# Attention in a fused kernel: scores in batches of four blocks instead of two, with the matmul banks divided anew and the row sums moved by ScalarE

## The chip, the cores and the metric

The kernel runs on one core of a Trainium2 chip. The metric is the device time of the whole program in microseconds (us). The engines are named as the profile names them: PE is TensorE (matmuls), DVE is VectorE, ACT is ScalarE, POOL is GpSimd, and SP issues most DMA transfers. Each engine works through its own instructions in program order and waits for the others by semaphores.

## The reference, cut to what matters

```
scores = (1/8) * q @ k^T               # 2 batches, 12 heads, 448 rows, 64 wide
scores = cap * tanh(scores / cap)
attn   = exp(scores - max) / (sum(exp(scores - max)) + 1e-9)
x      = attn @ v                      # as 896 rows of 768
x      = relu(x @ w_in)^2 @ w_out      # 768 -> 2048 -> 768
out    = silu(x @ w2_in) @ w2_out
```

In the path that runs here the cap bounds the scores, so no maximum is taken off: exp is applied to cap * tanh as it is.

## The kernel before, in words

The program has two parts: the attention (about the first 87 us) and two feed-forward layers on the result. The order of the attention's instructions is written out in one loop of `attention_bounded`; the feed-forward's comes from a planner with costs and due times, and is the same instruction list in both kernels.

Heads go in pairs. Pair i = 2m + b is the two heads of head-pair m in batch b, so there are 12 pairs and 6 values of m. Keys are cut in blocks: for each m there are A0, A1, A2 (128 keys each of pair 2m), B0, B1, B2 (the same of pair 2m + 1) and C (the last 64 keys of both pairs). These are 42 blocks, in the order A0 A1 A2 C B0 B1 B2 for m = 0 to 5. For each block

- `scores` (L640) makes the transposed scores in two banks of PSUM (one per head), and ACT applies tanh to both, 128 x 896 numbers, into a tile e (L648; eight such tiles);
- ACT applies exp in place (L744);
- `values` (L659) multiplies by v and adds up over the four blocks of a pair in a bank px;
- `add` (L673, L675, L679) adds the e tiles of a pair on DVE into a tile total.

When a pair is complete, DVE copies px to its cell x_c (L701, `evacuate`). When both pairs of an m are, PE sums the two totals over the keys with a matmul against ones (L687, `add_up`), DVE copies those sums out (L705), and they go through DMA: to 32 partitions (L708), inverted on DVE (L711, L712), written to a scratch in HBM (L713) and fetched back spread out (L719). Then DVE multiplies the cell by them (L724, `normalise`) and POOL splits the cell at once into two float16 parts, high (L1531) and low (L1532), in the tile x0f. The last two pairs, 10 and 11, take a shorter way: PE makes their sums spread out already (L696, tiles sump), and DVE adds, inverts and multiplies (L731 to L733, `last_sums`).

The loop takes two blocks per step h: scores and tanh of the two, exp of the two, then on DVE and PE the adds and values of the two blocks before. A list `todo` holds the later steps of the sums with the step at which they are due. In between, `ws.step()` issues the preparation of feed-forward weights (L360 to L393).

[...] Before, four are two pairs of banks for scores and four are single banks shared by px and the sums.

The feed-forward begins with `plain`, whose first product ha_0f reads batch 0 of x0f. Its loops run over `r` (two halves), the parts (high by high, high by low, low by high) and the cells; for batch 0 they read the cells in this order: c0 and c4 (six matmuls), then c2 and c6 (six matmuls), with weights hl_0, then the same with hl_1 and the same for batch 1 (ha_1f: c1, c5, c3, c7). c8 and c10 come after these 48 matmuls. So the eighth matmul of ha_0f is the first to read the high part of c6, and the tenth the first to read its low part.

Of the kernel before, what the change touches and what calls it, by code (L numbers as in the profile page):

```python
# [26 lines left out]
def softcap_attention_relu2_silu(  # L27
# [47 lines left out]
    work = ctx.enter_context(tc.tile_pool(name="work", bufs=1))  # L75
    psum = ctx.enter_context(tc.tile_pool(name="psum", bufs=2, space=PSUM))

    dram = ctx.enter_context(tc.tile_pool(name="dram", bufs=1, space=bass.MemoryType.DRAM))

    def bank(name):  # L80
        return psum.tile([128, 512], F32, tag="p", bufs=4, name=name)
# [7 lines left out]
    ib, ip = idle.bitcast(BF16), bank("idle")  # L89
    for _ in range(20):  # L90
        nc.tensor.matmul(ip[:, :256], lhsT=ib[:, :128], rhs=ib[:, :256], start=True, stop=True)

# [507 lines left out]
    def attention_bounded(att, spool, ws, x0):  # L600
# [21 lines left out]
        scratch = dram.tile([NH, S], F32, tag="scratch", name="scratch")  # L622
        ex, total, px, sums, st, rb = {}, {}, {}, {}, {}, {}

# [9 lines left out]
        def scores(m, x):  # L634
            sp = bank2(spool, f"s{m}_{x}")
# [12 lines left out]
            nc.scalar.activation(t, sp[:, :, :S], AF.Tanh, scale=scale_s)  # L648

        def values(m, x):  # L650
            for i in (2 * m, 2 * m + 1) if x == "C" else (pair_of(m, x),):
                if i not in px:
                    px[i] = bank(f"px{i}")
            e = ex[m, x]
            for b in range(2) if x == "C" else (None,):
                for j in range(2):
# [5 lines left out]
                        rhs=e[:, j] if b is None else e[head(b), j],  # L662
                        start=x == "A0" or b == 1,
                        stop=x == "B2" or b == 0,
                    )

        def add(m, x):
            e, i = ex[m, x], None if x == "C" else pair_of(m, x)
            if i == NP2 - 1:
                return  # L670
            if x in ("A1", "B1"):
# [4 lines left out]
            if x in ("C", "B1"):  # L676
                b = int(x == "B1")
                t = total[2 * m + b][head(b)]
                nc.vector.tensor_tensor(t, t, ex[m, "C"][head(b)], op=ALU.add)  # L679

        def add_up(m):

            s = sums[m] = bank(f"sum{m}")
            for b in range(2):
# [6 lines left out]
        def add_up_pair(i, t, start=True, stop=True, part=slice(0, 128)):  # L691

            if start:
                sums["p", i] = bank(f"sump{i}")
            for j in range(2):
# [40 lines left out]
        todo, last = [], 2 * NQ - 2  # L736
        loads = {0: 0, 2: 1, 4: 2, 7: 3, 11: 4, 16: 5}
        groups = [blocks[n : n + 2] for n in range(0, len(blocks), 2)]
        for h in range(len(groups) + 1):
            if h < len(groups):  # L740
                for m, x in groups[h]:
                    scores(m, x)
                for m, x in groups[h]:
                    nc.scalar.activation(ex[m, x], ex[m, x], AF.Exp, scale=scale_c)  # L744
                for m, x in groups[h]:
                    if x in ("A0", "B0"):
                        i = pair_of(m, x)
                        if i + 2 < NP2:
                            pr.load_v(i + 2)
                    if x in ("A1", "C") and m + 1 < NQ:  # L750
                        pr.load(2 * m + 2 + (x == "C"))
            if h == 1:
# [4 lines left out]
                nc.vector.tensor_scalar(gcap, gcap, 1e-9 * ONE, None, op0=ALU.mult)  # L757
            older = groups[h - 2] if h > 1 else []
            for m, x in older:
                if x in ("C", "B2"):  # L760
                    evacuate(2 * m + (x == "B2"))
            for m, x in groups[h - 1] if h else []:
                add(m, x)
            for m, x in groups[h - 1] if h else []:
                values(m, x)
            for m, x in groups[h - 1] if h else []:
                if m == NQ - 1 and x in ("C", "B0", "B1", "B2"):
                    add_up_pair(
                        last + 1, ex[m, x], x == "C", x == "B2", head(1) if x == "C" else slice(0, 128)
                    )  # L770
                if m == NQ - 1 and x == "C":
                    add_up_pair(last, total[last])
            for m, x in older:
# [7 lines left out]
            if h in loads:  # L781
                ws.load_to(loads[h])
            for f, at in list(todo):
                if h >= at:
                    f()
                    todo.remove((f, at))
            if 5 <= h < 17:
                ws.step()
        for st_ in last_sums(last):
            st_.fn()  # L790
        for f, _ in todo:
# [4 lines left out]
    def attention_general(att, spool, ws, x0):  # L796
# [8 lines left out]
        for i in range(NP2):  # L805
            pr.load(i)
            pr.load_whole_v(i)
            for j in range(2):
# [7 lines left out]
                for g in range(2):  # L816
                    sp = bank2(spool, f"sg{n}_{g}")
                    for e in range(2):
# [786 lines left out]
    def run(attention, tag, dt):  # L1605
        narrow = dt == F16
        power = POWER if narrow else dict.fromkeys(POWER, 0)
        with ExitStack() as pools:
# [25 lines left out]
            with (  # L1634
                tc.tile_pool(name=f"att{tag}", bufs=2) as att,
                tc.tile_pool(name=f"s{tag}", bufs=2, space=PSUM) as spool,
            ):
                attention(att, spool, ws, x0)
            qpool = pools.enter_context(tc.tile_pool(name=f"q{tag}", bufs=4, space=PSUM))
# [65 lines left out]
```

## Time and profile before

| | us |
|---|---|
| median of 3 runs | 495.69 (495.53 to 495.81) |
| profiled execution: its time | 496.47 |
| profiled execution: span of the trace | 494.70 |
| busy in the span: PE, DVE, ACT | 484.2, 427.2, 363.9 |

The span runs from the first to the last event in the trace. The 1.77 us between it and the execution's time lie around it. PE is busy 98% of the span, but that share counts a matmul as busy from its issue to its modelled end, so small pauses between matmuls of different shapes lie inside it.

### The profile page before, as it was taken

What the parts mean: (1) busy time and instruction counts of PE and PEld (TensorE: products, weight loads), DVE (VectorE), ACT (ScalarE), POOL (GpSimd) and SP (SyncE); (2) the same over time, 40 slices, a digit from 0 to 9 for tenths busy, and PEclk for the clock granted to TensorE, in tenths of its full rate; (3) what the DMA queues carried; (4) which work ended last, traced back from release to release, by engine and by line L of the source; (5) the groups of instructions that cost most, each with busy time, mean ns of one, the idle gap of its engine ahead of it and who ended that gap; (6) DMA issues with size and microseconds to landing.
All of it is one profiled execution on the core that took longest, in us unless ns stands there. A gap on an engine that the chain in (4) does not pass through costs nothing.

```text
span 494.7 us, 7120 instructions
## 1 busy us (share of the span) xinstructions
PE 484.2 (98%) x2563; PEld 233.5 (47%) x2563; DVE 427.2 (86%) x772; ACT 363.9 (74%) x592; POOL 49.2 (10%) x46
## 2 busy tenths in 40 slices
PE   8999999999999999999999999999999999998995
PEld 4323333455555555555555554555555445554552
DVE  0778998998999998999998999999967799988663
ACT  5999996899979935999987878779754689871100
POOL 1001555302002000112200000100010000000000
PEclk9999999999999999999999999999999999999998
DMA  7746561343653113337751333303745733033024
GB/s 246 280 133 164 182 197 30 91 161 134 204 192 129 64 65 127 130 127 237 273 192 64 129 128 129 97 32 127 259 180 152 272 130 127 1 112 112 1 78 154
DMA packets 22386, 69.76 MB, mean 141 GB/s; under 512 B 2886, under 2 KB 14150, under 8 KB 22342
## 3 DMA queue, kind: packets, MB, share of 16 engines
q1 hardware_dynamic: 22308, 69.22, 42.3%
q8 instruction: 22, 0.36, 0.3%
q14 instruction: 22, 0.18, 0.1%
q0 software_dynamic: 32, 0.00, 0.0%
q10 hardware_dynamic: 2, 0.00, 0.0%
HBM read 63.64 MB, written 5.54 MB: 140 GB/s over the span
## 4 chain that ended last, share of the span: by engine, by line
PE 92%; ACT 3%; DMA 2%; DVE 1%; issue 0%; SPq 0%; ACTq 0%
PE p_0df L932 8%; PE px L659 7%; PE p_6df L932 4%; PE p_2bf L932 4%; PE s_B L640 3%; PE s_A L640 3%; PE ha_0f L932 3%; PE yb_5f L932 3%; PE yb_0f L932 3%; PE yb_1f L932 3%; PE yb_3f L932 3%; PE yb_4f L932 3%; PE yb_2f L932 3%; PE ha_1f L932 3%; PE p_4df L932 2%; DMA yf<-spill 2%
## 5 line engine op out<-in xcount | busy, mean ns | idle before, releaser
L648 ACT ACTIVATE e_A<-s_A 128x896 f32<-128x896 f32 x18 | 15.9, 918 | 4.7 <-PE s_A L640 4.5
L648 ACT ACTIVATE e_B<-s_B 128x896 f32<-128x896 f32 x18 | 15.9, 917 | 3.9 <-PE s_B L640 3.6
L744 ACT ACTIVATE e_B<-e_B 128x896 f32<-128x896 f32 x18 | 16.5, 953 | 0.0
L744 ACT ACTIVATE e_A<-e_A 128x896 f32<-128x896 f32 x18 | 16.5, 954 | 0.0
L1434 DVE SCALAR_TENSOR_TENSOR yf<-p_6df,yf 128x448 f32<-128x448 f32 x15 | 9.2, 623 | 6.1 <-PE p_6df L932 6.1
L679 DVE TENSOR_TENSOR total<-total,e_C 64x896 f32<-64x896 f32 x11 | 12.9, 1173 | 0.4
L882 DVE TENSOR_TENSOR yaf<-p_2bf,yaf 128x448 f32<-128x448 f32 x15 | 9.3, 621 | 1.1 <-PE p_2bf L932 1.0
L1434 DVE SCALAR_TENSOR_TENSOR yf<-p_4df,yf 128x448 f32<-128x448 f32 x15 | 9.1, 618 | 0.0
L391 ACT ACTIVATE hl_107f<-u_86f 128x768 f16<-128x768 f32 x1 | 0.8, 843 | 11.1 <-DVE u_86f L416 11.1
L218 DVE SCALAR_TENSOR_TENSOR x1f<-yaf,x1f 128x448 f16<-128x448 f32 x12 | 7.4, 620 | 1.5 <-ACT x1f L871 1.5
L675 DVE TENSOR_TENSOR total<-total,e_A 128x896 f32<-128x896 f32 x6 | 8.2, 1359 | 0.3
L882 DVE TENSOR_TENSOR yaf<-yaf 128x448 f32<-128x448 f32 x12 | 7.1, 621 | 1.1 <-ACT yaf L871 1.0
L673 DVE TENSOR_TENSOR total<-e_A,e_A 128x896 f32<-128x896 f32 x6 | 7.4, 1242 | 0.4 <-ACT e_A L744 0.4
L871 ACT ACTIVATE x1f<-yaf 128x448 f16<-128x448 f32 x12 | 6.8, 570 | 0.7 <-DVE yaf L882 0.5
L360 POOL CAST zeros<-raw_wd_2f 128x768 f16<-128x768 bf16 x1 | 1.1, 1056 | 63.1 <-DVE u_55f L365 63.1
L757 DVE TENSOR_SCALAR gcap<-gcap 128x1 f32<-128x1 f32 x1 | 0.2, 154 | 7.6 <-ACT gcap L756 7.6
L673 DVE TENSOR_TENSOR total<-e_B,e_B 128x896 f32<-128x896 f32 x5 | 6.5, 1294 | 0.0
L1434 DVE SCALAR_TENSOR_TENSOR yf<-c_6df,yf 128x448 f32<-128x448 f32 x3 | 1.9, 624 | 4.9 <-PE c_6df L932 4.9
L391 ACT ACTIVATE hr_50f<-u_66f 128x384 f16<-128x384 f32 x1 | 0.5, 522 | 7.5 <-PE p_0df L932 7.5
L732 DVE RECIPROCAL r<-r 128x448 f32<-128x448 f32 x2 | 5.9, 2953 | 0.1
L675 DVE TENSOR_TENSOR total<-total,e_B 128x896 f32<-128x896 f32 x5 | 5.5, 1091 | 0.4
L360 POOL CAST zerosf<-raw_wa15f 128x768 f16<-128x768 bf16 x1 | 1.3, 1329 | 45.1 <-DVE u_27f L365 45.1
(1808 smaller groups left out, 1676.0 us busy)
## 6 DMA issues: line engine op xcount, KB each, us to landing
yf<-spill SPq DMA_DIRECT2D x12, 224.0 KB, 4.8
out<-yf SPq DMA_DIRECT2D x12, 224.0 KB, 2.2
rb<-scratch SPq DMA_DIRECT2D x10, 224.0 KB, 4.5
raw_wb_0f<-in_moe_w_out SPq DMA_DIRECT2D x2, 768.0 KB, 5.7
raw_wb_1f<-in_moe_w_out SPq DMA_DIRECT2D x2, 768.0 KB, 4.3
raw_wb_2f<-in_moe_w_out SPq DMA_DIRECT2D x2, 768.0 KB
raw_wb_3f<-in_moe_w_out SPq DMA_DIRECT2D x2, 768.0 KB, 5.0
raw_wb_4f<-in_moe_w_out SPq DMA_DIRECT2D x2, 768.0 KB, 4.2
```

Source lines behind the costliest of these rows:

```text
L218: nc.vector.scalar_tensor_tensor(lo, x, scale, hi, op0=ALU.mult, op1=ALU.subtract, accum_out=watch.low() if see else None)
L640: nc.tensor.matmul(sp[:, j, :S] if b is None else sp[head(b), j, :S], lhsT=qk[head(j), 1, 128 * c : min(128 * c + 128, S)], rhs=qk[head(j) ...
L648: nc.scalar.activation(t, sp[:, :, :S], AF.Tanh, scale=scale_s)
L659: nc.tensor.matmul(px[i][head(j), :S], lhsT=v_m[:, 3 * j + int(x[1])] if b is None else pr.vc[m][head(b), j], rhs=e[:, j] if b is None els ...
L673: nc.vector.tensor_tensor(t, ex[m, x[0] + "0"], e, op=ALU.add)
L675: nc.vector.tensor_tensor(total[i], total[i], e, op=ALU.add)
L679: nc.vector.tensor_tensor(t, t, ex[m, "C"][head(b)], op=ALU.add)
L744: nc.scalar.activation(ex[m, x], ex[m, x], AF.Exp, scale=scale_c)
L871: return Step("A", cols, lambda: nc.scalar.activation(at(out), at(src), func, scale=scale), list(deps))
L882: return Step(eng, cols, lambda: e.tensor_tensor(at(out), at(x), at(y), op=op), list(deps))
L932: nc.tensor.matmul(acc, lhsT=w(e_w, kk), rhs=x(e_x, kk), start=first and i == 0, stop=last and i == len(n) - 1, skip_group_check=more,)
L1434: st = Step("D", S + 95 * see, lambda: nc.vector.scalar_tensor_tensor(yb, acc, to_y, yb, op0=ALU.mult, op1=ALU.add, accum_out=watch.low() ...
```

## The change

1. The 42 blocks go in batches of 2, 2, 2, 2, then 4 six times, then 2 five times, instead of 21 batches of 2. In a batch, C is put last.
2. The banks: three pairs of banks that scores and the sums of `add_up` take in turn, and two banks for px.
3. The sums of an m are copied out by ACT (L724 of the new kernel, `evacuate_sums`), no longer by DVE, and `add_up` stands right behind the scores of a batch instead of behind the values.
4. Due times are counted in blocks, not steps; v is loaded behind the values, not ahead; the sums of pairs 10 and 11 share one pair of banks, and the DVE steps of pair 10 (`evacuate`, `last_sums`) stand in the last step but one.

```diff
-    def bank2(spool, name):
-        return spool.tile([128, 2, 512], F32, tag="s", bufs=2, name=name)
+    def bank2(spool, name, n=1):
+        return spool.tile([128, 2, 512], F32, tag="s", bufs=n, name=name)
+    def next_banks(spools, name):
+        spools.append(spools.pop(0))
+        return bank2(spools[-1], name)
...
-            s = sums[m] = bank(f"sum{m}")
+            s = sums[m] = next_banks(spool, f"sum{m}")[:, 0]
...
-            nc.vector.tensor_copy(t, sums.pop(m)[:, :S])
+            nc.scalar.activation(t, sums.pop(m)[:, :S], AF.Copy)
...
-        groups = [blocks[n : n + 2] for n in range(0, len(blocks), 2)]
+        sizes = [2] * 4 + [4] * 6 + [2] * 5
+        groups = [blocks[sum(sizes[:n]) : sum(sizes[: n + 1])] for n in range(len(sizes))]
+        groups = [sorted(gr, key=lambda e: e[1] == "C") for gr in groups]
...
+            at = sum(sizes[:h])
             if h < len(groups):
                 for m, x in groups[h]:
                     scores(m, x)
+                for m, x in older:
+                    if x == "B2":
+                        add_up(m)
+                        evacuate_sums(m)
+                        todo.append((lambda m=m: invert(m), at + 2))
+                        todo.append((lambda m=m: fetch(m), at + 4))
+                        for b in range(2):
+                            todo.append((lambda i=2 * m + b: normalise(i), at + 10 + 2 * b))
                 for m, x in groups[h]:
                     nc.scalar.activation(ex[m, x], ex[m, x], AF.Exp, scale=scale_c)
...
-            for m, x in older:
-                if x == "B2":
-                    add_up(m)
-                    evacuate_sums(m)
-                    todo.append((lambda m=m: invert(m), h + 1))
-                    todo.append((lambda m=m: fetch(m), h + 2))
-                    for b in range(2):
-                        todo.append((lambda i=2 * m + b: normalise(i), h + 4 + 2 * b))
...
+            if h == first_late + 1:
+                evacuate(last)
+                del left[last]
+                for st_ in last_sums(last):
+                    st_.fn()
-        for st_ in last_sums(last):
-            st_.fn()
         for f, _ in todo:
             f()
...
+                psum.append((ppool, 2 if narrow else 4))
+                spools = [
+                    banks.enter_context(tc.tile_pool(name=f"s{n_}{tag}", bufs=1 if narrow else 2, space=PSUM))
+                    for n_ in range(3 if narrow else 1)
+                ]
```

On PE, at the first batch of four (blocks A1, A2 of m = 1 and what follows; s_ are scores, px_ values, sum_ the sums). Before:

```order
L640 MATMUL s_A_256<-qk2f 128x448 x2
L640 MATMUL s_A_261<-qk2f 128x448 x2
L659 MATMUL px_225<-e_B_235,vt1f 64x448 x2
L659 MATMUL px_274<-e_A_240,vt2f 64x448 x2
L640 MATMUL s_C<-qk2f 64x448
L640 MATMUL s_C<-qk3f 64x448
L640 MATMUL s_C<-qk2f 64x448
L640 MATMUL s_C<-qk3f 64x448
L640 MATMUL s_B_286<-qk3f 128x448 x2
```

and in the changed kernel, at the same place (from the score of A2 of m = 1 on; that of A1 stands right ahead of it):

```order
L649 MATMUL s_A_267<-qk2f 128x448 x2
L649 MATMUL s_B_272<-qk3f 128x448 x2
L649 MATMUL s_C<-qk2f 64x448
L649 MATMUL s_C<-qk3f 64x448
L649 MATMUL s_C<-qk2f 64x448
L649 MATMUL s_C<-qk3f 64x448
L672 MATMUL px_233<-e_B_243,vt1f 64x448 x2
L672 MATMUL px_297<-e_A_248,vt2f 64x448 x2
L649 MATMUL s_B_307<-qk3f 128x448 x2
L649 MATMUL s_B_312<-qk3f 128x448 x2
L649 MATMUL s_A_317<-qk4f 128x448 x2
L649 MATMUL s_A_322<-qk4f 128x448 x2
```

The scores of two later blocks have moved ahead of the values of the two blocks before, and four scores stand in a row behind them; s_A_322 is the second block of m = 2.

On DVE, at the end of the attention (x_c are the cells, rb the inverted sums from HBM, sump and sums_late the sums of pairs 10 and 11, r their inverses). Before:

```order
L724 TENSOR_TENSOR x_c6f<-x_c6f,rb_686 128x448
L679 TENSOR_TENSOR total_725<-total_725,e_C 64x896
L711 TENSOR_SCALAR st_739<-st_739,gcap 32x56
L712 RECIPROCAL st_739<-st_739 32x56
L701 COPY x_c10f<-px_704 128x448
L724 TENSOR_TENSOR x_c7f<-x_c7f,rb_686 128x448
L731 TENSOR_SCALAR r_790<-sump_767,gcap 128x448
L732 RECIPROCAL r_790<-r_790 128x448
L733 TENSOR_TENSOR x_c10f<-x_c10f,r_790 128x448
L724 TENSOR_TENSOR x_c8f<-x_c8f,rb_787 128x448
```

and in the changed kernel:

```order
L698 TENSOR_TENSOR total_738<-total_738,e_C 64x896
L743 TENSOR_TENSOR x_c5f<-x_c5f,rb_663 128x448
L730 TENSOR_SCALAR st_733<-st_733,gcap 32x56
L731 RECIPROCAL st_733<-st_733 32x56
L720 COPY x_c10f<-px_708 128x448
L750 TENSOR_SCALAR r_782<-sums_late,gcap 128x448
L751 RECIPROCAL r_782<-r_782 128x448
L752 TENSOR_TENSOR x_c10f<-x_c10f,r_782 128x448
L743 TENSOR_TENSOR x_c6f<-x_c6f,rb_711 128x448
L743 TENSOR_TENSOR x_c7f<-x_c7f,rb_711 128x448
L743 TENSOR_TENSOR x_c8f<-x_c8f,rb_797 128x448
```

The multiplications of cells c6 and c7 stood ahead of the inversion for pair 10 and stand behind it now.

On PE, the last instructions of the attention. Before:

```order
L696 MATMUL sump_764<-e_C,ones 64x448 x2
L696 MATMUL sump_767<-total_725,ones 64x448 x2
L696 MATMUL sump_764<-e_B_720,ones 64x448 x2
L659 MATMUL px_757<-e_B_747,vt11f 64x448 x2
L659 MATMUL px_757<-e_B_752,vt11f 64x448 x2
```

and in the changed kernel:

```order
L715 MATMUL sums_late<-e_B_717,ones 64x448 x2
L715 MATMUL sums_late<-e_C,ones 64x448 x2
L715 MATMUL sums_late<-total_738,ones 64x448 x2
L672 MATMUL px_762<-e_B_752,vt11f 64x448 x2
L672 MATMUL px_762<-e_B_757,vt11f 64x448 x2
L715 MATMUL sums_late<-e_B_752,ones 64x448 x2
L715 MATMUL sums_late<-e_B_757,ones 64x448 x2
L970 LDWEIGHTS hl_0f
```

The sum of pair 10 (from its total) is now the last of three, and two blocks of values and two of sums stand between it and the feed-forward's first matmul.

## Rows read from the trace of the kernel before

**Rows 1.** Windows: busy us (and instructions) of PE, PEld, DVE, ACT, POOL; clock; DMA

```profile
60.00:80.00 20.00, 20.00 (x118) 6.18 (x116) 19.52 (x25) 18.08 (x22) 9.65 (x8) 1.00 0.50 147
```

**Rows 2.** The chain that ended last, by time: start us, us, what

```profile
18.69 1.71 PE s_A L640 x8
20.39 1.65 PE px L659 x8
22.05 0.91 PE s_C L640 x8
22.96 0.95 PE s_B L640 x4
...
25.57 0.89 PE sum L687 x8
...
84.39 1.50 PE px L659 x8
...
92.04 4.54 PE ha_1f L932 x24
```

**Rows 3.** Timeline of ACT: start us, us, instruction, count

```profile
20.73 1.74 ACT L648 ACTIVATE e_A<-s_A 128x896 f32<-128x896 f32 x2
...
24.00 0.95 ACT L648 ACTIVATE e_C<-s_C 128x896 f32<-128x896 f32 x1
...
85.94 0.54 ACT L793 ACTIVATE x_c11f<-px 128x448 f32<-128x448 f32 x1 [3.22 <-PE px L659]
86.38 0.57 ACT L247 ACTIVATE junk<-hl_0f 128x448 bf16<-128x448 f16 x1
```

**Rows 4.** Timeline of PE at the end of the attention

```profile
83.47 0.92 PE L696 MATMUL sump<-e_B,ones 128*64 128x448 f32 x4
84.22 1.67 PE L659 MATMUL px<-e_B,vt11f 128*64 128x448 f32 x8
...
87.33 2.44 PE L932 MATMUL ha_0f<-x0f,hl_0f 128*128 128x448 f16 x12
```

**Rows 5.** Timeline of DVE at the end of the attention

```profile
82.24 0.62 DVE L724 TENSOR_TENSOR x_c7f<-x_c7f,rb 128x448 f32<-128x448 f32 x1
83.69 0.68 DVE L731 TENSOR_SCALAR r<-sump,gcap 128x448 f32<-128x448 f32 x1 [0.83 <-PE sump L696]
...
87.39 0.62 DVE L733 TENSOR_TENSOR x_c10f<-x_c10f,r 128x448 f32<-128x448 f32 x1
88.55 0.62 DVE L724 TENSOR_TENSOR x_c8f<-x_c8f,rb 128x448 f32<-128x448 f32 x1 [0.53 <-DMA rb<-scratch]
89.09 0.62 DVE L724 TENSOR_TENSOR x_c9f<-x_c9f,rb 128x448 f32<-128x448 f32 x1
```

**Rows 6.** Timeline of POOL at the end of the attention

```profile
82.94 0.57 POOL L1531 TENSOR_SCALAR x0f<-x_c7f 128x448 f16<-128x448 f32 x1 [0.57 <-DVE x_c7f L724]
83.59 1.04 POOL L1532 TENSOR_TENSOR x0f<-x_c7f,x0f 128x448 f16<-128x448 f32 x1
89.26 0.87 POOL L1531 TENSOR_SCALAR x0f<-x_c8f 128x448 f16<-128x448 f32 x1 [4.63 <-DVE x_c8f L724]
90.22 1.29 POOL L1532 TENSOR_TENSOR x0f<-x_c8f,x0f 128x448 f16<-128x448 f32 x1
```

**Rows 7.** Groups by line: busy us, mean ns, idle before

```profile
L705 DVE COPY sm<-sum 128x448 f32<-128x448 f32 x5 | 3.1, 617 | 2.2 <-PE sum L687 2.2
L675 DVE TENSOR_TENSOR total<-total,e_B 128x896 f32<-128x896 f32 x5 | 5.5, 1091 | 0.4
```

**Rows 8.** Waits of PE in the whole span: us in total, times, longest

```profile
PE p_4df L932 <- DVE yf L1434: 1.4, 1, 1.4
...
PE s_A L640 <- ACT e_A L648: 0.3, 1, 0.3
```

**Rows 9.** Window behind PE's longest wait, columns as in rows 1

```profile
454.20:458.00 3.80, 3.80 (x21) 1.97 (x21) 3.80 (x10) 1.69 (x2) 0.00 (x0) 1.00 0.00 0
```

**Rows 10.** DMA issues: KB each, median us from issue to landing

```profile
qk9f<-in_k SPq DMA_DIRECT2D x1, 224.0 KB, 7.0
```

More of the change, by code (lines that the diff above doesn't have):

```diff
@@ L622, in attention_bounded @@
         scratch = dram.tile([NH, S], F32, tag="scratch", name="scratch")
-        ex, total, px, sums, st, rb = {}, {}, {}, {}, {}, {}
+        ex, total, px, sums, st, rb, left, added = {}, {}, {}, {}, {}, {}, {}, set()
         NQ = NP2 // 2
@@ L634, in scores @@
         def scores(m, x):
-            sp = bank2(spool, f"s{m}_{x}")
+            sp = next_banks(spool, f"s{m}_{x}")
             for j in range(2):
@@ L650, in values @@
         def values(m, x):
+            fresh, ended = {}, {}
             for i in (2 * m, 2 * m + 1) if x == "C" else (pair_of(m, x),):
-                if i not in px:
+                fresh[i] = i not in px
+                if fresh[i]:
                     px[i] = bank(f"px{i}")
+                left[i] = left.get(i, 4) - 1
+                ended[i] = left[i] == 0
             e = ex[m, x]
@@ L662, in values @@
                         rhs=e[:, j] if b is None else e[head(b), j],
-                        start=x == "A0" or b == 1,
-                        stop=x == "B2" or b == 0,
+                        start=fresh[i],
+                        stop=ended[i],
                     )
@@ L670, in add @@
                 return
+            for b in range(2) if x == "C" else ():
+                if 2 * m + b in total:
+                    rest_of(m, b)
             if x in ("A1", "B1"):
@@ L693, in add_up_pair @@
             if start:
-                sums["p", i] = bank(f"sump{i}")
+                sums["p", i] = late_sums[0][:, i - last]
             for j in range(2):
@@ L736, in attention_bounded @@
         todo, last = [], 2 * NQ - 2
-        loads = {0: 0, 2: 1, 4: 2, 7: 3, 11: 4, 16: 5}
-        groups = [blocks[n : n + 2] for n in range(0, len(blocks), 2)]
-        for h in range(len(groups) + 1):
+        loads = {0: 0, 4: 1, 8: 2, 14: 3, 22: 4, 32: 5}
+        sizes = [2] * 4 + [4] * 6 + [2] * 5
+        groups = [blocks[sum(sizes[:n]) : sum(sizes[: n + 1])] for n in range(len(sizes))]
+        groups = [sorted(gr, key=lambda e: e[1] == "C") for gr in groups]
+        first_late = next(n for n, gr in enumerate(groups) if {(NQ - 1, "C"), (NQ - 1, "B0")} & {*gr})
+        late_sums, lasting = [], spool[0]
+        for h in range(len(groups) + 1):
+            if h == first_late + 1:
+                while spool[0] is not lasting:
+                    spool.append(spool.pop(0))
+                late_sums.append(next_banks(spool, "sums_late"))
+            before, older = groups[h - 1] if h else [], groups[h - 2] if h > 1 else []
+            here = range(sum(sizes[:h]), sum(sizes[: h + 1]))
+            at = sum(sizes[:h])
             if h < len(groups):
@@ L757, in attention_bounded @@
                 nc.vector.tensor_scalar(gcap, gcap, 1e-9 * ONE, None, op0=ALU.mult)
-            older = groups[h - 2] if h > 1 else []
-            for m, x in older:
-                if x in ("C", "B2"):
-                    evacuate(2 * m + (x == "B2"))
-            for m, x in groups[h - 1] if h else []:
+            for i, n in list(left.items()):
+                if n == 0:
+                    evacuate(i)
+                    del left[i]
+            steps = len({*here} & {*range(10, 34, 2)})
+            for n, (m, x) in enumerate(before):
                 add(m, x)
-            for m, x in groups[h - 1] if h else []:
+                if n == 1 and steps > 1:
+                    ws.step()
+                    steps -= 1
+            for m, x in before:
                 values(m, x)
-            for m, x in groups[h - 1] if h else []:
+            for m, x in before:
+                if x in ("A0", "B0"):
+                    i = pair_of(m, x)
+                    if i + 2 < NP2:
+                        pr.load_v(i + 2)
+            for m, x in before:
                 if m == NQ - 1 and x in ("C", "B0", "B1", "B2"):
                     add_up_pair(
-                        last + 1, ex[m, x], x == "C", x == "B2", head(1) if x == "C" else slice(0, 128)
+                        last + 1, ex[m, x], ("p", last + 1) not in sums, x == "B2", head(1) if x == "C" else slice(0, 128)
                     )
@@ L772, in attention_bounded @@
                     add_up_pair(last, total[last])
[L773 to L790 removed]
+            for n in here:
+                if n in loads:
+                    ws.load_to(loads[n])
+            for f, due in list(todo):
+                if at >= due:
+                    f()
+                    todo.remove((f, due))
+            ws.step(steps)
+            if h == first_late + 1:
+                evacuate(last)
+                del left[last]
+                for st_ in last_sums(last):
+                    st_.fn()
         for f, _ in todo:
```

36 lines of the change are left out of this document (20 added, 16 removed).

## Prediction

> **What bounds the kernel now.** I read the chain that ended last first. It is PE nearly from end to end, and in the attention it is an unbroken row of s, px and sum pieces [rows 2]. The list of PE's waits says the same: in the attention PE waits once, 0.3 us behind the first tanh, and the longest wait of the whole span is 1.4 us, near the end [rows 8]. So any time that PE saves in the attention comes off the end, unless it then waits for somebody. The window of the later attention shows who is next: DVE 19.52 us and ACT 18.08 us of 20.00 [rows 1]. Neither has room for much.
>
> In the chain one reads what PE loses between matmuls. Two blocks of scores take 1.71 us and one takes 0.95, so a further block costs 0.76 and the start of a run of scores 0.19 or 0.20. Two blocks of px take 1.65 us, but 1.50 where they follow matmuls of the same array shape, sump [rows 2], so the start of a px run costs 0.15. A block C costs 0.91 and a sum 0.89 wherever they stand [rows 2].
>
> **What the change saves on PE.** Matmuls are neither added nor removed, only regrouped. Counted through the order of both kernels, up to the first ha_0f, runs of scores fall from 20 to 14 and runs of 128-row px or sum matmuls from 21 to 16; C and sum pieces stay at 6 + 6 and 5. That is 6 x 0.20 + 5 x 0.15 = **1.95 us saved**. The 0.3 us wait in the first step [rows 8] goes, since a third pair of banks is free. But px then arrives that much earlier at the first exp, which is no earlier, so I count nothing.
>
> **What the first batch of four costs.** ACT is back to back there. The tanh of block A1 of m = 1, the ninth block, starts at 20.73, and a pair of blocks takes 24.00 - 20.73 = 3.27 us [rows 3]. With batches of four, ACT does tanh, tanh, tanh, tanh and then four exps before it takes the thirteenth block: it starts that tanh at 20.73 + 2 x 3.27 = 27.27 and is done with it about 0.95 later, at 28.2. PE comes to the ninth block at 18.69 [rows 2]. It then has three scores (0.20 + 3 x 0.76 = 2.48), C (0.91), two px (1.65), and three scores (2.48): it is through at 26.2. The next score needs the bank pair of the thirteenth block, free at 28.2. With three pairs for batches of four that is a wait of 2.0 us, or 2.1 with the signal; part of it may already fall on C of that batch, the sum is the same. Bounds: 1.6 (if ACT does a pair in 3.2) and 2.5 (in 3.4). Later batches should not wait: one of four with a C needs 2.48 + 0.91 + 0.15 + 3 x 0.75 + 0.91 = 6.7 us on PE, 7.6 with a sum; ACT needs 6.54, or 7.0 with the copy of a sum. So ACT gains on PE from there on. **Attention: -1.95 + 2.1 = +0.15 us**, bounds -0.35 and +0.55.
>
> **Edits that I cost at nothing.** The five copies of sums leave DVE (3.1 us of it [rows 7]) and go to ACT at 0.44 each, from the start of one such copy to the next instruction [rows 3]: 2.2 us, covered by the gain of ACT on PE above. Without that cover it would be up to 2.2. DVE was nowhere awaited, so its 3.1 us give nothing directly. With four score blocks in the air, a tanh needs an e tile that DVE and PE have read two batches earlier: eight tiles are two batches, and DVE has been relieved. px has two banks instead of a share of four, and a new pair's px waits for DVE's copy; the copies stand first in DVE's work of a step, and I take 0 (price below). On SP, the loads of q and k for the next m now stand behind a transfer that waits for ACT's copy of the sums, and v is loaded a batch later. A load has some six blocks of PE's time (about 1.9 us each) and took 7.0 us at the slow end [rows 10]; I take 0.
>
> **What stands late at the hand-over.** This is the term that decides. Call E the moment at which the sum of pair 10 leaves PE, 83.47 before [rows 4]. *PE:* in the new order two blocks of px and two of sums follow, then ha_0f. In the trace that stretch is 84.22 to 87.33 [rows 4], 3.11 us. A product of 448 columns takes 4.54 / 24 = 0.19 us [rows 2], so PE wants the low part of c6, in its tenth product, at E + 3.11 + 9 x 0.19 = E + 4.8, and the high part in its eighth at E + 4.4. *DVE:* before, c6 had been multiplied long before. Now c6 stands behind the inversion for pair 10. That chain starts at 83.69 = E + 0.22, the multiplication of c10 at 87.39 = E + 3.92, and the next one 0.54 later (88.55 to 89.09) [rows 5]: c6 is multiplied from E + 4.46. *POOL:* from the start of such a multiplication to the end of the low part took 88.55 to 91.51 = 2.96 us for c8, with DVE busy on the next cell, and 82.24 to 84.63 = 2.39 us for c7, with DVE idle [rows 5, 6]. DVE goes on with c7, c8 and c9, so c8 is the nearer row. The low part is ready at E + 7.42, with the signal E + 7.5. **PE waits 7.5 - 4.8 = 2.7 us**, first some 1.7 for the high part and then 1.0 for the low one. Bounds: 2.1 by the row of c7; 3.2 if both POOL steps stretch as c8's longer ones again. The wait does not depend on when E is: both sides count from it. Cells c7, c8 and c9 come 1.7 to 2.2 us after each other and are wanted 4.5 us and more later, so they cost nothing.
>
> [...]
>
> **The sum.** 496.47 for the profiled execution, +0.15 and +2.7, is 499.3. The median lies 0.78 under the profiled execution, so I expect a median of **498.5 us**, slower by 0.6%. With all bounds: 1.75 to 3.75 us more, 497.4 to 499.4. Within 0.2%, about 1.0 us, a measurement of this kernel cannot tell from no change.
>
> **Rivals.**
> *A, the forecast:* 498.5; chance 0.62.
> *B, the hand-over is covered, no change:* this is the other side. It holds if c6 is not read so early, for example if ha_0f's wait on POOL is met by earlier cells and c6 is read with c8 and c10, nine us after ha_0f begins. For it: the trace names only a tile x0f, not its cells. Against it: the loops give c0, c4, c2, c6. Then the attention's +0.15 is left: 495.8. It decides as soon as PE's wait for c6 falls below 0.9 us. Chance 0.14. *F,* the same and ACT also not the pace of the first batch of four: 495.69 - 1.95 = 493.7; against it stands that ACT is back to back there. Chance 0.07.
> *C, px waits for DVE as well:* two banks for px mean that the first px of a pair waits for the copy of the one two before it. If DVE is an addition behind (1.09 us [rows 7]) at two of the twelve pairs, that is 2.2 us on top: 500.7. For it: DVE at 19.52 of 20 [rows 1]. Against: 3.1 us are taken off DVE. A load from SP that comes late would cost the same 1 to 2 us. Chance 0.12.
> *D, the clock falls after the wait:* PE pauses 1.7 and 1.0 us within 3 us. If its clock then fell to the lower level for the next 24 products, these would take twice 4.54 us: +4.5 at most, half of that as a middle, 500.8. After the pause of 1.4 us the granted clock stands at 1.00 [rows 8, 9], so little speaks for it. [...] Chance 0.05.
>
> **How the numbers follow.** Slower by over 0.2%: A, C and D, 0.79. The same: B, 0.14. Faster: F, 0.07. For the range I take A with its bounds, B at the low end and the nearer half of C: 495.7 to 500.4. The forecast's own range is 497.4 to 499.4.
>
> **What would show it.** In the changed kernel the list of PE's waits should have ha_0f behind POOL's x0f of c6, some 2.7 us in two waits, at the first ten products. Around 21 to 28 us a score should wait for ACT's tanh, some 2.1 us in all. Runs of four px or scores in the chain should cost 0.75 a block with one start. ha_0f should begin about where it did (87.3, within 0.6). DVE's multiplication of c6 should start about 0.5 us behind that of c10. ACT should have no idle before its tanhs between 7 and 45 us. The forecast is wrong if ha_0f starts at 85.5 (then ACT was not the pace), if no wait stands at its tenth product, or if px waits for DVE's copies.

## The result and the profile after

The changed kernel is slower: 498.68 us, the median of 5 runs (497.80 to 500.41), against 495.65 us, the median of 5 runs of the kernel before beside it (495.37 to 495.81). The ratio is 1.0063, with a 95% interval of 1.0048 to 1.0077. The forecast was 498.5, in a range from 495.7 to 500.4. The profiled execution took 500.41 us, with a span of 498.6 us; that of before took 496.47.

The waits of PE are read first (us in total, times, longest):

```profile
PE s_A L649 <- ACT e_B L657: 1.5, 1, 1.5
PE ha_0f L970 <- POOL x0f L1569: 1.5, 1, 1.5
...
PE ha_0f L970 <- POOL x0f L1570: 0.8, 1, 0.8
...
PE s_C L649 <- ACT e_A L657: 0.4, 1, 0.4
```

Against [rows 8], four waits are new. Two are in the first batch of four, for ACT's tanh. Two are at ha_0f, for POOL: L1569 makes the high part of a cell, L1570 the low one. The timeline of PE shows where they lie:

```profile
18.32 1.77 PE L649 MATMUL s_A<-qk2f 64*128 64x448 f32 x8
...
21.23 0.59 PE L649 MATMUL s_C<-qk2f 64*64 64x448 f32 x1 [0.39 <-ACT e_A L657]
...
23.80 1.77 PE L649 MATMUL s_B<-qk3f 64*128 64x448 f32 x8
...
27.82 1.02 PE L649 MATMUL s_A<-qk4f 64*128 64x448 f32 x4 [1.49 <-ACT e_B L657]
28.77 0.96 PE L706 MATMUL sum<-total,ones 128*32 128x448 f32 x8
...
84.18 1.67 PE L672 MATMUL px<-e_B,vt11f 128*64 128x448 f32 x8
...
87.29 1.50 PE L970 MATMUL ha_0f<-x0f,hl_0f 128*128 128x448 f16 x7
90.27 0.54 PE L970 MATMUL ha_0f<-x0f,hl_0f 128*128 128x448 f16 x2 [1.49 <-POOL x0f L1569]
91.64 1.28 PE L970 MATMUL ha_0f<-x0f,hl_0f 128*128 128x448 f16 x3 [0.83 <-POOL x0f L1570]
92.71 3.45 PE L970 MATMUL ha_0f<-x0f,hl_1f 128*128 128x448 f16 x12
96.00 1.30 PE L970 MATMUL ha_1f<-x0f,hl_0f 128*128 128x448 f16 x6
...
105.08 2.43 PE L970 MATMUL ha_0f<-x0f,hl_2f 128*128 128x448 f16 x12
```

ha_0f begins at 87.29, where it began before (87.33, [rows 4]); nearly the whole loss lies behind it. Seven products run, the eighth and ninth wait, the tenth waits again. A product takes 0.19 us, so the eighth was due at 87.29 + 7 x 0.19 = 88.61 and began at 90.27, which is 1.66 late; the tenth was due at 90.65 and began at 91.64, 0.99 late. That is 2.65 us. (The brackets show 1.49 and 0.83: they count from the listed ends, 88.79 and 90.81, which lie 0.18 and 0.16 behind the times due.)

Then comes a surprise. The next twelve products, which took 2.43 in the kernel before, take 3.45 here. The windows show why (busy us and instructions of PE, PEld, DVE, ACT, POOL; then the granted clock, the DMA share and GB/s):

```profile
91.00:92.00 1.00, 0.36 (x2) 0.14 (x2) 1.00 (x2) 1.00 (x3) 1.00 (x2) 0.68 0.00 0
...
93.00:94.00 1.00, 1.00 (x4) 0.44 (x3) 0.97 (x2) 0.97 (x3) 1.00 (x2) 0.50 0.00 0
...
95.00:96.00 1.00, 1.00 (x8) 0.49 (x5) 1.00 (x1) 0.99 (x2) 1.00 (x2) 1.00 0.00 0
```

The granted clock falls about when PE goes on (a mean of 0.68 from 91 to 92 us). It then stands at 0.50 while PE is busy, and is back at 1.00 from 95 us. In the kernel before, the run of products from 87.33 went through at 2.28 us for each twelve. Here the 24 from ha_0f's begin to ha_1f's took 96.00 - 87.29 = 8.71 us instead of 4.54: 2.65 of it are the waits, and the other 1.52 the clock.

Who was late is read from DVE and POOL:

```profile
85.12 2.95 DVE L751 RECIPROCAL r<-r 128x448 f32<-128x448 f32 x1
88.10 0.62 DVE L752 TENSOR_TENSOR x_c10f<-x_c10f,r 128x448 f32<-128x448 f32 x1
88.65 0.62 DVE L743 TENSOR_TENSOR x_c6f<-x_c6f,rb 128x448 f32<-128x448 f32 x1
```

```profile
89.35 0.87 POOL L1569 TENSOR_SCALAR x0f<-x_c6f 128x448 f16<-128x448 f32 x1 [6.01 <-DVE x_c6f L743]
90.31 1.28 POOL L1570 TENSOR_TENSOR x0f<-x_c6f,x0f 128x448 f16<-128x448 f32 x1
```

c6 stands behind the inversion and the multiplication of c10. POOL idles 6.01 us for it, begins with it at 89.35 and ends the low part at 91.59; PE goes on at 91.64.

### The profile page after: what moved, and what is told of

The parts are those of the page before. It is cut to its first block, busy times and chain, and to the rows that moved or that the text cites. A ratio compares the mean times of both kernels' runs of the same rounds, so it can differ in the third digit from the quotient of the medians.

```text
span 498.6 us, 7114 instructions
## 1 busy us (share of the span) xinstructions
PE 484.4 (97%) x2563; PEld 235.0 (47%) x2563; DVE 427.1 (86%) x767; ACT 366.1 (73%) x597; POOL 51.6 (10%) x46
## 4 chain that ended last, share of the span: by engine, by line
PE 87%; ACT 6%; DVE 2%; DMA 2%; issue 1%; POOL 0%; SPq 0%; DVEq 0%; ACTq 0%
PE p_0df L970 8%; PE px L672 5%; PE p_6df L970 4%; PE p_2bf L970 4%; PE yb_5f L970 3%; PE yb_1f L970 3%; PE yb_4f L970 3%; PE ha_1f L970 3%; PE yb_2f L970 3%; PE yb_0f L970 3%; PE yb_3f L970 3%; PE ha_0f L970 3%; PE s_A L649 2%; PE p_4df L970 2%; PE s_B L649 2%; DMA yf<-spill 2%
## 5 line engine op out<-in xcount | busy, mean ns | idle before, releaser
L691 DVE TENSOR_TENSOR total<-total,e_A 128x896 f32<-128x896 f32 x6 | 6.5, 1088 | 0.5
L970 PE MATMUL ha_0f<-x0f,hl_0f 128*128 128x448 f16 x18 | 4.6, 388 | 2.3 <-POOL x0f L1569 1.5
L970 PEld LDWEIGHTS <-hl_0f 128*128 128x128 f16 x36 | 3.5, 99 | 6.6 <-issue 3.8
```

The lines of the kernel that those rows point to most:

```text
L970: nc.tensor.matmul(acc, lhsT=w(e_w, kk), rhs=x(e_x, kk), start=first and i == 0, stop=last and i == len(n) - 1, skip_group_check=more,)
```

## The experiments

All profiles are compared from one mark: the first px matmul. It comes between 9.21 and 10.09 us, for reasons that lie ahead of it (experiment 7), and everything behind it on PE moves along. Two distances are read: from the first px to ha_0f (the attention), and to the first product with hl_2f, 72 products later (attention and hand-over). The last column is the timed ratio less one, times the median of before beside it.

| kernel | first px | ha_0f | hl_2f | attention, against before | hand-over too | timed (95%) |
|---|---|---|---|---|---|---|
| before | 10.09 | 87.33 | 100.96 | 0 | 0 | |
| 7: before again | 9.21 | 86.45 | 100.08 | 0.00 | 0.00 | |
| changed | 9.79 | 87.29 | 105.08 | +0.26 | +4.42 | +3.1 (2.4, 3.8) |
| 1: c6 early | 9.60 | 86.89 | 101.09 | +0.05 | +0.62 | +0.8 (0.3, 1.3) |
| 2: before, c6 late | 9.81 | 87.12 | 102.64 | +0.07 | +1.96 | +1.9 (1.2, 2.6) |
| 3: waits filled | 9.47 | 86.84 | 103.12 | +0.13 | +2.78 | +2.5 (1.7, 3.2) |
| 4: c6 early, other sizes | 9.68 | 85.67 | 99.68 | -1.25 | -0.87 | -0.5 (-1.0, 0.0) |
| 5: batches of two | 9.94 | 87.33 | 100.97 | +0.15 | +0.16 | 0.0 (-0.4, 0.5) |
| 6: copies on DVE | 9.47 | 93.70 | 108.27 | +6.99 | +7.93 | +7.3 (6.5, 8.0) |
| 8: next cell by DVE | 9.53 | 85.52 | 99.55 | -1.25 | -0.85 | -0.2 (-0.7, 0.2) |
| 9: changed again | 9.91 | 87.79 | 105.74 | +0.64 | +4.96 | +3.1 (2.2, 4.1) |
| 10: next cell earlier | 9.47 | 85.46 | 99.73 | -1.25 | -0.61 | -0.8 (-1.3, -0.3) |

In experiment 9 the mark is not clean: its first px waits 0.25 us for an exp, so ACT, which paces the first batch of four, is late against PE from the start.

**1. c6 multiplied early.** One number of the changed kernel: the due time of the multiplications for m = 3.

```diff
-todo.append((lambda i=2 * m + b: normalise(i), at + 10 + 2 * b))
+todo.append((lambda i=2 * m + b: normalise(i), at + (8 if m == 3 else 10) + 2 * b))
```

> The changed kernel, but DVE multiplies c6 ahead of the inversion for pair 10 instead of behind it; everything else as in the change. Hand-over theory: the two waits of ha_0f for POOL's x0f (1.66 + 0.99 us in the profile after) are gone, the granted clock stays at 1.00 from 90 to 96 us, ha_0f still begins at about 87.3, and the time is that of the kernel before, 495.7 (495.2 to 496.2). Rival, the loss lies in the batches of four themselves (banks, ACT's copies, late loads): the waits go, but the time stays at 498 or more, and ha_0f begins later than 88.

Measured: 496.83 us against 495.82, ratio 1.0016 (1.0006 to 1.0027). The hand-over theory holds: both waits for POOL are gone, the clock stays at 1.00, and some 2 us come back. The rival falls, as ha_0f begins at 86.89. But 0.8 us remain, more than expected. On PE:

```profile
86.89 2.44 PE L970 MATMUL ha_0f<-x0f,hl_0f 128*128 128x448 f16 x12
...
99.58 0.54 PE L970 MATMUL ha_1f<-x0f,hl_0f 128*128 128x448 f16 x2 [0.41 <-DVE x0f L227]
```

A cell that was hidden behind c6 is late now. It is c11, on DVE:

```profile
96.07 0.62 DVE L752 TENSOR_TENSOR x_c11f<-x_c11f,r 128x448 f32<-128x448 f32 x1
...
98.03 0.95 DVE L374 SCALAR_TENSOR_TENSOR u_4f<-raw_wb_0f,zeros 128x768 int32<-128x768 int32 x1
98.90 0.62 DVE L227 SCALAR_TENSOR_TENSOR x0f<-x_c11f,x0f 128x448 f16<-128x448 f32 x1
```

PE's rows put the cost at 0.62 - 0.05 = 0.57 us. In the kernel before, the same step of c11 lay earlier:

```profile
97.06 0.62 DVE L218 SCALAR_TENSOR_TENSOR x0f<-x_c11f,x0f 128x448 f16<-128x448 f32 x1
```

That is 97.06 - 87.33 = 9.73 us behind ha_0f, against 98.90 - 86.89 = 12.01 here. So this too is a cost of the change's order: the sum of pair 10 leaves PE nearer to ha_0f (3.11 us ahead of it instead of 3.86 [rows 4]), and the multiplications of c7, c8 and c9 stand between the two inversions, where only those of c8 and c9 stood [rows 5].

**2. c6 late in the kernel before.** The batches of two stay; only the multiplications for m = 3 go behind the inversion.

```diff
-todo.append((lambda i=2 * m + b: normalise(i), h + 4 + 2 * b))
+todo.append((lambda i=2 * m + b: normalise(i), 99 if m == 3 else h + 4 + 2 * b))
```

> The kernel before with this one thing of the change: c6 (and c7) multiplied by DVE behind the inversion for the last pair; the batches of two, the banks and the copies stay as they were. Hand-over theory: PE waits some 2.7 us at the eighth and tenth product of ha_0f, and loses 0 to 1.5 us more if the clock falls behind it: 498.3 to 499.9. Rival, the late multiplication alone does not delay PE: 495.7.

Measured: 497.79 us, ratio 1.0038 (1.0025 to 1.0052), less than expected. The late multiplication alone does delay PE:

```profile
87.12 1.50 PE L932 MATMUL ha_0f<-x0f,hl_0f 128*128 128x448 f16 x7
89.36 0.54 PE L932 MATMUL ha_0f<-x0f,hl_0f 128*128 128x448 f16 x2 [0.74 <-POOL x0f L1531]
90.72 0.73 PE L932 MATMUL ha_0f<-x0f,hl_0f 128*128 128x448 f16 x3 [0.82 <-POOL x0f L1532]
```

By PE's rows it is 1.96 - 0.07 = 1.89 us. The expectation used the 2.7 us of the prediction, and these hold for the order of the changed kernel alone. With batches of two, one more run of sump matmuls stands between the sum of pair 10 and ha_0f (83.47 to 84.22 in [rows 4], 0.75 us), and DVE's inversion gets that head start: 2.65 - 0.75 = 1.90. After these shorter pauses the clock stayed at 1.00 in the profile.

**3. The wait filled.** In the changed kernel 8 products stand ahead of the seventh and 4 ahead of the tenth of ha_0f; they write into the bank that ha_1f overwrites later. c6 is as late as before.

```diff
+def pad(k):
+    for _ in range(k):
+        nc.tensor.matmul(
+            accs[1, 0], lhsT=hl[:, 0, :128], rhs=self.x.form("p1", 0, 0),
+            start=True, stop=True,
+        )
...
+fill={0: lambda: pad(8), 3: lambda: pad(4)} if padded else {},
```

> The changed kernel, with 8 extra products ahead of the 7th or 8th and 4 ahead of the 10th of the first ha_0f; they write to the bank that the next accumulator overwrites later, so no result needs them and PE is busy while it would wait. c6 comes as late as before. Theory that the fall of the clock is a consequence of the pause and costs about 1.5 us in an execution that has it: no wait over 0.5 us is left there, the clock stays at 1.00 from 90 to 96 us, the next run of products (ha_1f) begins about 1.5 us earlier than in the profile after (94.5 against 96.0), and the time is about 497.6 with a small spread between runs. Rival, the clock falls there for another reason: a row of 0.50 or 0.6 still stands between 91 and 95 us, and the time is 498.7 or, if the extra products cost more than the wait, above it.

Measured: 498.54 us, ratio 1.0050 (1.0034 to 1.0065). In the profile the picture is the one that the theory asks for:

```profile
87.99 1.68 PE L1140 MATMUL ha_0f<-x0f,hl_0f 128*128 128x448 f16 x8
...
90.21 0.92 PE L1140 MATMUL ha_0f<-x0f,hl_0f 128*128 128x448 f16 x4
...
94.04 2.43 PE L972 MATMUL ha_1f<-x0f,hl_0f 128*128 128x448 f16 x12
```

The clock is 1.00 in every window from 90 to 95 us. ha_1f begins 94.04 - 86.84 = 7.20 behind ha_0f, against 8.71 in the changed kernel and 4.54 before: the delay of 2.65 us is there as before, within a hundredth, and 1.51 us of clock are gone. The expected gain in time did not come, though; the median is within 0.2 us of the changed kernel's. Experiment 9 takes that up, and shows that one profile without the fall cannot prove that the filling prevented it.

**4. The batches grown later.** The kernel of experiment 1, with the sizes below.

```diff
-sizes = [2] * 4 + [4] * 6 + [2] * 5
+sizes = [2] * 8 + [4] + [3] * 6 + [2] * 2
```

> The changed kernel with c6 multiplied early, and other sizes of batch: eight of two, one of four, six of three, two of two, so that the larger batches begin only where ACT has gained on PE. Theory that the 1.95 us of saved run starts were eaten by the wait for ACT's tanh in the first batch of four (1.5 + 0.4 us in the profile after): that wait falls under 0.5 us, ha_0f begins at about 86 instead of 87.3, and the time is about 494.2 (493.8 to 495.0). Rival, starts of runs are not worth time here, or another engine sets the pace of the whole attention: ha_0f begins at 87.3 again and the time is 495.7.

Measured: 495.41 us, ratio 0.9990 (0.9980 to 1.0000). No wait for a tanh is left in the list, and from the first px (9.68) to ha_0f it is 75.99 us instead of 77.24:

```profile
85.67 2.44 PE L970 MATMUL ha_0f<-x0f,hl_0f 128*128 128x448 f16 x12
```

The theory holds for the attention: the run starts are worth time once no early batch of four eats it, 1.3 us between experiments 1 and 4. The time is 1.2 us higher than expected: c11 takes back 0.38 of the 1.25, and the estimate had been made from ha_0f's absolute time.

**5. Batches of two in the new banks.** The changed kernel with sizes of two, so that the banks, ACT's copies and the later loads are left. (c6 then falls ahead of the inversion, c7 behind.)

```diff
-sizes = [2] * 4 + [4] * 6 + [2] * 5
+sizes = [2] * 21
```

> The changed kernel with batches of two throughout (sizes of 2, 21 times), so that only the banks, the sum copies on ACT and the later loads are left of the change; c6 is then multiplied ahead of the inversion again. Theory that these parts cost nothing: ha_0f begins at 87.3 within 0.3, no wait of PE over 0.5 us in the attention, and the time is that of before, 495.8 (495.3 to 496.3). Rival, the two banks for px, ACT's copies or the loads behind them cost PE time and the regrouping hides it: ha_0f at 88 or later and 496.8 or more, as the kernel with c6 early had (496.83 where its profile showed PE only 0.1 later than before).

Measured: 496.15 us against 495.91, ratio 1.0001 (0.9991 to 1.0010). The parts other than the regrouping cost nothing that the times can tell. By PE's rows it is 0.16 us; "What PE saves" below says from what.

**6. The copies of sums back on DVE.** The kernel of experiment 1 with one line as it was.

```diff
-nc.scalar.activation(t, sums.pop(m)[:, :S], AF.Copy)
+nc.vector.tensor_copy(t, sums.pop(m)[:, :S])
```

> The changed kernel with c6 early and with the five copies of sums back on DVE. Theory that neither engine is awaited for them: ha_0f begins at 86.9 within 0.3 as in the kernel with c6 early, the time is its 496.8 within 0.5. Rival, the 3.1 us taken off DVE are needed there: PE waits for DVE (px banks, e tiles) and ha_0f comes 1 us or more later; or, the other way, ACT's 2.2 us of copies lengthen the wait for the tanh: ha_0f comes 0.5 us or more earlier.

Measured: 503.27 us, ratio 1.0147 (1.0131 to 1.0162): 6.4 us more than the same kernel with the copies on ACT. The theory that nobody waits for them falls. PE's waits:

```profile
PE s_C L649 <- ACT e_A L657: 2.0, 2, 1.7
...
PE px L672 <- DVE x_c6f L720: 1.5, 1, 1.5
PE px L672 <- DVE x_c5f L720: 1.3, 1, 1.3
```

On DVE, and then on PE, around the second of these px waits:

```profile
60.05 0.62 DVE L724 COPY sm<-sum 128x448 f32<-128x448 f32 x1 [1.21 <-PE sum L706]
60.59 0.61 DVE L720 COPY x_c5f<-px 128x448 f32<-128x448 f32 x1
```

```profile
61.26 0.97 PE L672 MATMUL px<-e_B,vt7f 128*64 128x448 f32 x4 [1.28 <-DVE x_c5f L720]
```

The copy is 0.62 us long, but it waits for PE's sum, which stands behind a whole batch of scores; DVE's copy of px is queued behind it; and PE's next px needs that bank, as there are only two. PE waits for DVE, which waited for PE. The wait of 1.7 us behind ACT's tanh has the same origin, further back. On DVE and on ACT:

```profile
29.41 0.62 DVE L724 COPY sm<-sum 128x448 f32<-128x448 f32 x1 [8.70 <-PE sum L706]
```

```profile
31.66 0.92 ACT L657 ACTIVATE e_A<-s_A 128x896 f32<-128x896 f32 x1 [2.67 <-DVE total L689]
```

DVE stands 8.70 us at the first copy of a sum, its additions come late by that, and ACT stands 2.67 us for a tile e that they had not read yet.

**7. The kernel before, once more.** Unchanged.

> The kernel before, unchanged, for a second profile of it on this chip. It tells how far PE's rows differ between two executions: ha_0f at 87.3 within 0.3, and the wait for DVE's yf near the end (1.40 us in the first profile, 0.69 in the kernel with c6 early) either the same 1.4, and then it belongs to the kernel, or elsewhere between 0.7 and 1.7, and then it is scatter of the execution.

Measured: 495.26 us in one run. ha_0f begins 0.88 us earlier than in the first profile, outside of what was expected, but the distance from the first px is the same 77.24 us:

```profile
9.21 1.72 PE L659 MATMUL px<-e_A,vt0f 128*64 128x448 f32 x8
...
86.45 2.44 PE L932 MATMUL ha_0f<-x0f,hl_0f 128*128 128x448 f16 x12
```

What differs lies ahead of the mark. The 20 products that PE runs ahead of the first score took 4.45 us in the first profile and 3.88 here, and the first two blocks of scores 2.52 and 1.77:

```profile
5.43 2.52 PE L640 MATMUL s_A<-qk0f 64*128 64x448 f32 x8
```

```profile
4.87 1.77 PE L640 MATMUL s_A<-qk0f 64*128 64x448 f32 x8
```

So a single profile's absolute times carry nearly 1 us that is set in the first few us. PE's wait for yf near the end is 1.2 here, 1.4 in the first profile, and between 0.7 and 1.5 at its longest in the other kernels: scatter, as the second alternative had it.

**8. c11's high part on DVE.** The kernel of experiment 4, with the high part of c11 made by DVE instead of ACT. The planner then orders some later work otherwise.

```diff
 a.due = self.due[p, j] - 1.0
+if p == self.OWN[3] and j == 2 and self.y is None:
+    a.change()
```

> The kernel with c6 early and the batches grown later, and with the high part of c11 made by DVE right behind its multiplication, so that its low part comes ahead of a weight's unpacking (DVE has about 0.35 us more to do; the planner then orders some later work otherwise). Theory that c11 is what is late next: the wait of ha_1f for DVE's x0f (0.23 us in the list, 0.38 on PE's rows against before) is gone, PE stands 1.66 us ahead of before at 100 us instead of 1.28, and the time is 495.0. Rival, another wait takes its place: the time stays at 495.4 or rises with the changed order of later work.

Measured: 495.77 us, ratio 0.9995 (0.9985 to 1.0004). The wait for c11 is gone, but PE's lead at hl_2f is 0.85, as in experiment 4: a wait of 0.24 for ACT's copy of ha_0f has come in its place, and further on the reordered work adds waits, one of 0.4 for a weight among them. The rival holds.

**9. The changed kernel, once more.** Unchanged.

> The changed kernel, unchanged, for a second profile and more times with the mean granted clock of each. Theory that the fall of the clock after the waits is not part of every execution: in the first series three of five executions had a mean clock of 0.999 (497.8, 498.45, 498.68), which leaves no room for 3.4 us at 0.50, and the profiled one had 0.995 and the longest time, 500.41; so most executions here have a mean clock of 0.996 or more and lie at 497.8 to 498.9, and one with 0.995 or less lies 1.5 us above them. If this profile has no row of 0.50 or 0.62 between 91 and 95 us, ha_1f begins 2.65 us and not 4.1 us later than before, counted from the first px. Rival, the fall comes every time: 0.50 stands in this profile as well, and the times lie at 498.7 and above.

Measured: 499.41 us, the median of 6 runs, ratio 1.0063 (1.0044 to 1.0083). Its profile has the fall again:

```profile
93.00:94.00 1.00, 1.00 (x4) 0.46 (x3) 1.00 (x3) 0.91 (x3) 0.92 (x1) 0.50 0.00 0
```

From ha_0f to hl_2f it takes 105.74 - 87.79 = 17.95 us, against 13.63 before: 2.65 for the waits, as in the first profile, and 1.67 for the clock.

Not every execution can have it. Of both series together, six executions had a mean clock of 0.999: 497.80, 497.90, 498.45, 498.63, 498.68 and 499.00 us. A mean of 0.999 over some 497 us leaves room for about 1 us at 0.50, and the fall lasts over three: the windows from 91 to 95 us in the first profile (0.68, 0.50, 0.50, 0.62) make 3.4 us at 0.50. The other five had 0.995 or 0.996: 498.74, 499.82, 500.41, 500.76 and 500.92, among them the two profiled ones. (A low mean alone proves no fall there: the kernel before has 0.996 in some executions too, and in its profiled one, with 0.997, the clock falls behind the last products, with 0.50 from 492 us on. 498.74 may be such a case.) So four or five of eleven have the fall, and they lie some 2 us above the 498.54 in the middle of the others. The theory holds in that the fall is not part of every execution. It was wrong on the mean that would betray it: the profile with the fall has 0.996. This fits with experiment 3, which gained nothing at the median: its 498.54 is what the changed kernel takes without the fall. None of its six executions is above 499.25, so none looks like one with the fall; but six or seven of eleven of the changed kernel have none either, so it is likely, but not shown, that the filling prevents it.

**10. c11 ahead of a weight.** The kernel of experiment 4, with DVE's low part of c11 issued ahead of the unpacking u_4f, and all else in its order.

```diff
+if self.ahead and st.eng == "D" and self.ahead[0].deps[0].end is not None:
+    self.ahead[1] -= 1
+    if self.ahead[1] < 0 or st is self.ahead[0]:
+        self.ahead.pop(0).fn()
+        self.ahead = None
...
+if p == self.OWN[3] and j == 2 and self.y is None:
+    self.ws.ahead = [b, 0]
+    b.out_early = True
```

> The kernel with c6 early and the batches grown later, and with one instruction moved on DVE: the low part of c11 ahead of the unpacking of a weight instead of behind it; the order of all other work is that kernel's. Theory that c11 is the only thing late behind the attention there: PE's wait at ha_1f for DVE's x0f (0.23 us in the list, 0.38 by PE's rows) is gone, PE at 100 us and 300 us stands 1.25 us ahead of before, counted from the first px, instead of 0.87, and the time is 0.3 to 0.4 under that kernel's, about 0.9 to 1.2 under before (0.9975 to 0.998 of it). Rival, the unpacking is wanted next, so that the wait comes back at a later weight: 0.87 or less at 300 us and no change of time.

Measured: 494.94 us against 495.78, ratio 0.9983 (0.9973 to 0.9993). Its median is the lowest of the study, and it is faster than before. But the theory of its gain does not hold. The wait at ha_1f went, and PE's lead at hl_2f became 0.61 us instead of 0.87, and it is the same 0.61 at 300 us. On PE and on ACT:

```profile
99.73 2.43 PE L977 MATMUL ha_0f<-x0f,hl_2f 128*128 128x448 f16 x12 [0.48 <-ACT ha_0f L916]
```

```profile
98.23 1.07 ACT L371 ACTIVATE zeros<-raw_wb_1f 128x768 f16<-128x768 bf16 x1 [0.73 <-DVE u_4f L374]
99.17 1.55 ACT L916 ACTIVATE ha_0f<-ha_0f 128x448 f32<-128x448 f32 x3
```

The postponed u_4f delays ACT's next step, and ACT's copy of the first accumulators is queued behind that: the rival's mechanism, one instruction further. Whether this kernel differs from that of experiment 4 the timings cannot say, as their intervals overlap.

## Why the prediction was right, step by step

**What PE saves.** The chain of the changed kernel shows the new prices (start us, us, what):

```profile
36.42 3.16 PE px L672 x16
39.57 0.95 PE s_B L649 x4
40.53 2.25 PE s_A L649 x12
...
46.99 2.46 PE s_B L649 x12
```

Four px blocks take 3.16 = 0.15 + 4 x 0.75; three scores take 2.46 = 0.20 + 3 x 0.76, as the rows of before had said. That this is saving in time, and not only in busy time, experiments 4 and 5 show. Counted on PE up to ha_0f as the prediction counts, experiment 4 has 16 runs of scores and 18 of 128-row px or sum matmuls, instead of 20 and 21: 4 x 0.20 + 3 x 0.15 = 1.25 us, and the attention is 1.25 us shorter. Experiment 5 has 20 and 22, because the sum of a block C stands between two others there: 0.15 us more, and it is 0.15 us longer.

**The first batch of four.** Forecast 2.1 us (1.6 to 2.5). The brackets say 0.39 + 1.49 = 1.9; by due times, as for ha_0f, it is a little more. Three scores from 18.32 on would put C at 20.78, and it began at 21.23, which is 0.45 late. The fourth score of a run is due 3.20 - 0.76 = 2.44 behind the first (0.95 + 2.25 = 3.20 for four, in the chain above), so at 26.24, and it began at 27.82, 1.58 late. That is 2.0 us. The fourth then took 0.95 instead of 0.76, as the start of a run does. The step behind it can be checked on ACT:

```profile
20.25 1.74 ACT L657 ACTIVATE e_A<-s_A 128x896 f32<-128x896 f32 x2
...
26.80 1.77 ACT L657 ACTIVATE e_B<-s_B 128x896 f32<-128x896 f32 x2
```

From the ninth block's tanh to the thirteenth's it is 6.55 us; two pairs at 3.27 had given 6.54. ACT has no idle ahead of a tanh from 8 to 45 us, as expected. The attention came out at +0.26, forecast +0.15, and the terms add up: -1.95 + 2.03 + 0.19 = +0.27. In experiments 1 and 3 the wait at C is 0.22 and 0.13 us shorter (0.17 and 0.26 in the list), and so is the attention, with +0.05 and +0.13.

**The hand-over.** Forecast 2.7 us, 1.7 for the high part and 1.0 for the low; measured 1.66 + 0.99 = 2.65, and the same 2.65 in the second profile of the changed kernel and, with other work in the gap, in experiment 3. E, the moment at which the sum of pair 10 leaves PE, is 84.18. c6's multiplication was forecast for E + 4.46 and began at E + 4.47; the low part was to be ready at E + 7.42 and was at E + 7.41. From multiplication to low part it took 2.94 us, so the choice of the row of c8 (2.96) over that of c7 (2.39) was right: POOL's two steps took 0.87 and 1.28 with DVE at its next multiplications, as for c8 [rows 6]. (The prediction calls DVE idle at the row of c7. By [rows 5] it was so only up to 83.69, and then at the steps of pair 10; the low bound hangs on that row, the forecast does not.) Experiments 1 and 2 show the same cause from both sides: taken out of the changed kernel, the waits go; put into the kernel before, they come.

**What was costed at nothing.** It holds for this change: in experiment 5 the banks, the copies and the loads leave 0.01 us beside the 0.15 of the one more run. No px waits for DVE, no load comes late. The reasoning about the copies was too weak, though. It compared busy times, 3.1 us off DVE and 2.2 onto ACT, and called the first worth nothing. Experiment 6 shows that in this order of work the move is worth 6.4 us, because of what is queued behind a copy that waits: the copies of px and the additions.

**The rivals.** B falls: PE waits for c6 at the eighth and tenth product. F's condition does not hold in this kernel, since ACT is the pace of the first batch of four; experiment 4 shows that without such a wait the saved starts come off the attention in full. C falls: no px wait, no late load. D came true in part, and its chance of 0.05 was the wrong number of the prediction. The argument against it was one pause of 1.4 us with the clock at 1.00 behind it [rows 8, 9]. Behind two pauses of 1.66 and 0.99 us with two products between them, D's lower level did come in both profiles, 0.50 at 93 to 94 us, and by times and mean clocks it came in four or five of eleven executions. The cost was 1.5 and 1.7 us in the two profiles, less than the 2.25 taken as the middle. Behind the pauses of experiment 2, 1.89 us in all, the clock stayed at 1.00 in its profile, and so it did behind the single one of 1.58 us in the first batch of four.

**The sum.** For the profiled execution 499.3 was forecast, and 500.41 measured. The 1.1 us between them are the clock, 1.5, less the earlier first px, 0.3, and some 0.1 of the other terms. The median fits better (498.5 and 498.68), since three or four of the five executions had no fall. How near it came is in part luck: in experiment 9 half had the fall, and the median was 499.41.

## What to carry to other kernels

When a loop is regrouped, look at what the old grouping got done ahead of the next long instruction, and ask at which product of the next stage each result is read: here a multiplication of 0.62 us, put behind an inversion of 2.95 us, cost 2 to 4 us. Count an instruction that is moved to another engine by what stands behind it and what it waits for, not by its duration: here five copies of 0.62 us were worth 6.4 us. Larger batches save starts on the engine that is the bound, here 0.15 to 0.20 us each, but the first of them asks its partner for a lead that must have been built up, and without it cost 2.0 us here: let them grow only where the partner has gained on it.

## What the runs showed that was not expected

After waits of 1.66 and 0.99 us the granted clock fell to 0.50 for the next products, in both profiles of the changed kernel, and by times and mean clocks in four or five of its eleven executions; with filler products in the same gaps it stayed at 1.00 in the one execution profiled. Both profiles of the changed kernel have the fall, so no trace shows an execution with the waits and without it, and what decides between the two stays open.

The start of the attention moves by up to 0.9 us between executions of one kernel (first px at 9.21 and 10.09), while the 77.24 us behind it repeat to the hundredth. A mark inside the trace, and not the span, is what single profiles should be compared from.
